# Linear attention and squared-ReLU FFN on one core: softmax sums of four head pairs in one PSUM pair, their inverses spread by DMA from single rows

## The chip, the cores and the metric

The kernel runs on one core of a Trainium2 chip. The metric is the device time of one execution in microseconds. Before the change it is 482.66 us, the median of three runs (481.07 to 483.11).

## The reference

Attention with keys and values projected along the sequence from 1024 to 64 rows, and then a feed-forward layer with a squared ReLU. There are 8 batches of 8 heads, 1024 tokens of 64 elements; 8192 tokens of 512 enter the second part.

```python
k_proj = np.einsum('ks,bhsd->bhkd', E, k)              # 64 rows instead of 1024
v_proj = np.einsum('ks,bhsd->bhkd', F, v)
scores = (1 / np.sqrt(64)) * np.matmul(q, k_proj.transpose(0, 1, 3, 2))
attn = np.exp(scores - scores.max(-1));  attn = attn / (attn.sum(-1) + 1e-9)
x = np.matmul(attn, v_proj)                            # to (8192, 512)
h = np.maximum(x @ w_in, 0.0)                          # 512 -> 2048
out = (h * h) @ w_out                                  # 2048 -> 512
```

## The kernel before

A batch is split into two chunks of 512 tokens. The feed-forward part is the bulk of the work. It multiplies 2x2 block matrices in seven products instead of eight, so sums of blocks are made on VectorE beforehand: of x (x_sum, by `sum_x`), of h (`s12`, `s4`, by `sum_h`), and of the weights once. In the steady state two generators run side by side. `firsts` issues, step by step, one of the seven products of a group (four matmuls of 256 columns, line 652), and `seconds` issues one quantum of the second layer of the chunk before (four matmuls of 256 columns, line 572). A batch has 56 such steps, 28 a chunk. TensorE's order is written by hand; the order of the other engines follows from a list scheduler that works with the buffers' release.

The attention of the next batch is put between these steps by a plan: `on(step, b, name)` puts a method of batch b's `Attention` at that step. Per batch it consists of

- `load_kv`, `load_q`: loads on GpSimd's queue, into one buffer each for K, V and Q
- `project` (line 254): 16 matmuls give k and v projections in one PSUM bank; two kp copies of 64 rows for each half and one half of vp go through VectorE, the other half of vp through ScalarE
- `transpose_k_dma`, `transpose_q_dma`: DMA transposes on SP's queue
- `scores` for each of four head pairs: four matmuls into a pair of PSUM banks, and one Exp on ScalarE gives e, 128x1024 bf16
- `sums_spread(pr)` (line 376), once for two head pairs: see below
- `values(pr)` (line 396): four matmuls into the PSUM pair, and two multiplications by rs on VectorE give xT.

In the steady state all of these share a single pair of PSUM banks (`turn["pairs"] = 1`), so each block must wait until the one before has been read. In `sums_spread` eight matmuls with a 64x32 block of ones sum e over the keys, for two head pairs; each sum comes out on 32 equal rows. Ln and then Exp(-x) on ScalarE give `inv`, 128x1024 f32. Eight DMAs on SP's queue, each of 32 rows of 4 KB, spread these rows to two tiles `rs` of 128x1024, one for a head pair, so that every one of the 64 rows of a head has its inverse. `inv` and `rs` share three buffers.

The same queue of SP carries the stores of the outputs (line 566, 256 KB each, from three buffers o_sb) and the transposes. The buffers u of `part_pool` keep partial products that ScalarE copies out of PSUM (line 544), five of them.

The plan of a batch, with t the step at which batch b's first chunk begins in the first layer's stream: scores 0 to 2 of batch b+2 at t+44, t+47 and t+53, the sums of pairs 0 and 1 at t+50, scores 3 at t+57, the sums of pairs 2 and 3 at t+59, and values at t+63, t+66, t+76 and t+79; `project` of batch b+2 at t+30. The first batches run in a different, plainer order, and batches 2 to 7 go through `sums_spread`.

Of the kernel before, what the change touches and what calls it, by code (L numbers as in the profile page):

```python
# [9 lines left out]
P = 128  # L10
F32 = mybir.dt.float32
BF16 = mybir.dt.bfloat16
# [3 lines left out]
LO, HI = slice(0, 64), slice(64, 128)  # L16
# [3 lines left out]
def kernel(  # L20
# [11 lines left out]
    nc = tc.nc  # L32

    B, H, S, D = q.shape
# [3 lines left out]
    DM = moe_w_out.shape[1]  # L38
# [6 lines left out]
    TCH = S // 2  # L45
# [10 lines left out]
    const_pool = ctx.enter_context(tc.tile_pool(name="const", bufs=1))  # L56
# [4 lines left out]
    soft_pool = ctx.enter_context(tc.tile_pool(name="soft", bufs=3))  # L61
    x_pool = ctx.enter_context(tc.tile_pool(name="x", bufs=2))
    form_pool = ctx.enter_context(tc.tile_pool(name="form", bufs=1))
    part_pool = ctx.enter_context(tc.tile_pool(name="part", bufs=5))
    out_pool = ctx.enter_context(tc.tile_pool(name="outp", bufs=3))
    psum = ctx.enter_context(tc.tile_pool(name="ps", bufs=1, space=bass.MemoryType.PSUM))
    turn = {"att": 0, "bank": 0, "pairs": 2}

# [6 lines left out]
    def att_psum():  # L75
        turn["att"] += 1
        return pair_psum(turn["att"] % turn["pairs"])

    def bank(shape=(P, 512), dtype=F32, n=None):
        if n is None:  # L80
            turn["bank"] += 1
            n = turn["bank"]
        return psum.tile(list(shape), dtype, tag=f"bank{n % 4}", name="ps_bank")
# [34 lines left out]
    nc.vector.memset(zeros[:], 0.0)  # L118
    ones = const_pool.tile([P, D], BF16, name="ones")
    nc.vector.memset(ones[:], 1.0)  # L120


    W_IN_PIECES = ((0, 2), (2, 4), (4, 8), (8, 12), (12, 16))
# [3 lines left out]
    for j, (lo, hi) in enumerate(W_IN_PIECES):  # L127
        t = wpool.tile([P, NCB, (hi - lo) * P], BF16, name=f"w_in_{lo}")
# [6 lines left out]
    for j in range(WP):  # L135
        if j == WP - 1:
            load(Q0[:, :, 4:8, :], tokens(q, 0, i=slice(4, 8)))
        t = wpool.tile([P, fn, DM], BF16, name=f"w_out_{j}")
# [81 lines left out]
    VALUE_QUADS = ((LO, 0, 0, LO), (HI, 0, 1, HI), (HI, 1, 1, LO), (LO, 1, 0, HI))  # L220

    class Attention:
# [31 lines left out]
        def project(self):  # L254
            ps = att_psum()[:, 0]
            for i in range(NI):
                f, l = i == 0, i == NI - 1
                nc.tensor.matmul(ps[LO, :], lhsT=ET[:, i, :], rhs=self.K[:, :, i, :], start=f, stop=l)
                nc.tensor.matmul(ps[HI, :], lhsT=FT[:, i, :], rhs=self.V[:, :, i, :], start=f, stop=l)
            for g in range(2):  # L260
                self.keep_k(ps[LO, g * C // 2:(g + 1) * C // 2], g)
            self.keep_v(ps[HI, :])
# [110 lines left out]
                    nc.vector.tensor_copy(rs[j][lack:lack + 32], rs[j][have:have + 32])  # L373
                self.rs[pr + j] = rs[j]

        def sums_spread(self, pr):

            ps = att_psum()
            for j in range(2):
                for o, par, a, r in VALUE_QUADS:  # L380
                    c = 32 * (2 * a + j)
                    nc.tensor.matmul(
                        ps[c:c + 32, par], lhsT=ones[r, 0:32], rhs=self.e[pr + j][r, par], start=True, stop=True
                    )
            inv = soft_pool.tile([P, 2, TCH], F32, tag="rs", name="inv")
            nc.scalar.activation(inv[:], ps[:], AF.Ln)
            nc.scalar.activation(inv[:], inv[:], AF.Exp, scale=-1.0)
            for j in range(2):
                rs = soft_pool.tile([P, 2, TCH], F32, tag="rs", name="rs")
                for a in range(2):  # L390
                    have = 32 * (2 * a + j)
                    for to in (64 * a, 64 * a + 32):
                        nc.sync.dma_start(rs[to:to + 32], inv[have:have + 32])
                self.rs[pr + j] = rs

        def values(self, pr, spare=False):

# [40 lines left out]
    class Chunk:  # L438
# [100 lines left out]
                        yield  # L539


        def keep(self, ps):
            u = part_pool.tile([P, DM], F32, name="u")
            nc.scalar.copy(u[:], ps)  # L544
            return u

# [31 lines left out]
        def second_spread(self, second_bank):  # L578
# [21 lines left out]
            yield  # L600
            yield from product(7, chain)
            self.put(1, 1, chain, p5)
            yield
            yield from product(3, other)
# [6 lines left out]
        def second_seven(self, first, chain, other, last=False):  # L611
# [16 lines left out]
            yield  # L628
            yield from product(7, chain)
            self.put(1, 1, chain, p5)  # L630
            yield
            yield from product(3, other)
# [10 lines left out]
    class Group:  # L643
# [35 lines left out]
        def p5(self):  # L679
            self.other = bank(n=turn["bank"] + 2)  # L680
            self.product(5, self.other, True)
            self.kept5 = self.chunk.keep(self.other[:])

        def p6(self):
            self.product(6, self.chain)
            self.u2 = self.chunk.keep(self.chain[:])

        def p2(self):
            self.product(2, self.first)
# [18 lines left out]
    with tc.manual_schedule(engines={PE}):  # L708
# [30 lines left out]
        def at(step, fn, *args, **kwargs):  # L739
            plan.setdefault(step, []).append(lambda: fn(*args, **kwargs))  # L740

        def run(steps, start=0):
            for step, _ in enumerate(steps, start + 1):
                for stage in plan.pop(step, []):
                    stage()
            return step

        def run_all(*parts):
            step = 0
            for part in parts:  # L750
                step = run(part, step)
            assert not plan, plan

        atts = {0: att}
        chunk = {(0, c): Chunk(att, c) for c in range(2)}
# [7 lines left out]
        nxt = atts[1]  # L763
# [42 lines left out]
        nxt = atts[2]  # L806
        at(1, nxt.transpose_k)
        at(3, nxt.scores, 0)
        at(5, nxt.scores, 1)
        at(7, nxt.sums_spread, 0)  # L810
        at(9, nxt.scores, 2)
        at(11, nxt.scores, 3)
        turn["pairs"] = 1
        run_all(chunk[1, 0].first_plain())
        lent.close()
        second_pool = ctx.enter_context(tc.tile_pool(name="ps_second", bufs=1, space=bass.MemoryType.PSUM))
# [37 lines left out]
        def both():  # L854
            f, s = firsts(), seconds()
            for _ in f:
                next(s, None)
                yield

        def on(step, b, name, *args):  # L860
            at(step, lambda: getattr(atts[b], name)(*args))

        for b in range(1, B - 1):
            t = 56 * (b - 1)
            if b > 1:
                on(t + 1, b + 1, "scores", 3)
            on(t + 3, b + 1, "sums_spread", 2)
            on(t + 7, b + 1, "values", 0)
            on(t + 10, b + 1, "values", 1)
            on(t + 20, b + 1, "values", 2)  # L870
            on(t + 23, b + 1, "values", 3)
            for c in range(2):
                at(t + 24, lambda b=b, c=c: chunk[b + 1, c].sum_x())
            if b + 2 < B:
                on(t + 2, b + 2, "transpose_q_dma")
                if b + 3 < B:
                    at(t + 2, begin, b + 3)
                    on(t + 3, b + 3, "load_q")
                on(t + 30, b + 2, "project")
                on(t + 32, b + 2, "transpose_k_dma")  # L880
                if b + 3 < B:
                    on(t + 34, b + 3, "load_kv")
                on(t + 44, b + 2, "scores", 0)
                on(t + 47, b + 2, "scores", 1)
                on(t + 50, b + 2, "sums_spread", 0)
                on(t + 53, b + 2, "scores", 2)
        steps = both()
        run(steps)
        assert not plan, plan
# [31 lines left out]
```

## Time and profile before

| | us |
|---|---|
| median of three runs | 482.66 |
| the profiled execution | 482.35 |
| its span | 480.5 |
| matmuls of the first layer's seven products, line 652, x_sum by w_in_sum (x624) | 93.9 |
| values, matmuls line 405 (x112) | 11.5 |
| scores, matmuls line 329 (x112) | 11.3 |
| copies of the projection on VectorE, lines 246 and 247 (x14 each) | 5.8 and 5.7 |
| copy of half of vp on VectorE, line 252 (x7) | 4.9 |
| multiplications into xT, line 409 (x56) | 36.0, 684 ns each |
| x_sum, four additions, line 150 | 417 and 418 ns each |

"Busy" is the time in which an engine has work; several matmuls can be under way together, so their sum says little, and the starts of neighbouring matmuls tell more. How much of the DMA engines' time the queues take:

```profile
q0 software_dynamic: 30640, 29.23, 39.4%
q1 hardware_dynamic: 49216, 36.97, 29.2%
```

The columns are packets, megabytes, and the share of 16 engines' span. q0 is GpSimd's loads, q1 all that SP issues.

### The profile page before, as it was taken

The page shows a single profiled execution, that of the slowest core. Times are in us where ns is not written, and L with a number is a line of the kernel's source. Part 1 is how long each engine was busy: PE and PEld are TensorE (multiplying, and loading weights), DVE is VectorE, ACT ScalarE, POOL GpSimd, SP SyncE. Part 2 cuts the span into 40 slices and gives each one's busy share as a digit, 9 for nine tenths or more (in the row PEclk, how much of TensorE's full clock was granted, in tenths as well). Part 3 has the DMA queues.
Part 4 walks back from the last instruction along what each step waited for, and adds up shares of the span by engine and source line. Part 5 has one row for each costly group of instructions (what it writes and reads, how often), then busy time and mean ns, then how long its engine had stood idle before and what let it go on. Part 6 is the DMA issues. An engine that isn't in the chain of part 4 may idle for free.

```text
span 480.5 us, 10027 instructions
## 1 busy us (share of the span) xinstructions
PE 470.4 (98%) x4106; PEld 351.5 (73%) x4106; DVE 350.7 (73%) x613; ACT 287.2 (60%) x466; POOL 32.4 (7%) x45
## 2 busy tenths in 40 slices
PE   8999999999999999999999999999999999999996
PEld 3444445537878788787878778887887778888885
DVE  2456897956996679767897579966797678967671
ACT  2464467397547774678546785477745775565641
POOL 7310010200010000100010000100000000000000
PEclk9999999999999999999999999999999999999999
DMA  9999998999949496767939499495811054101012
GB/s 184 204 205 206 221 164 150 168 230 189 197 86 168 122 201 163 119 134 186 196 103 182 93 220 175 96 160 139 203 56 55 23 132 111 67 23 67 24 65 89
DMA packets 80046, 66.98 MB, mean 139 GB/s; under 512 B 30720, under 2 KB 76032, under 8 KB 80000
## 3 DMA queue, kind: packets, MB, share of 16 engines
q0 software_dynamic: 30640, 29.23, 39.4%
q1 hardware_dynamic: 49216, 36.97, 29.2%
q8 instruction: 32, 0.52, 0.4%
q10 hardware_dynamic: 144, 0.13, 0.1%
q14 instruction: 14, 0.11, 0.1%
HBM read 59.24 MB, written 16.78 MB: 158 GB/s over the span
## 4 chain that ended last, share of the span: by engine, by line
PE 71%; DVE 22%; ACT 3%; issue 2%; DMA 1%; DVEq 0%; ACTq 0%
PE ps_bank L652 28%; PE ps_second L572 27%; PE ps_bank L489 6%; DVE h L150 3%; DVE x_sum L150 3%; DVE h L666 3%; DVE s L150 2%; PE ps_att L329 2%; DVE xT L409 2%; PE ps_second L549 2%; PE ps_att L405 2%; DVE kp L246 1%; DVE rs L373 1%; DVE kp L247 1%; DVE w_in_sum L150 1%
## 5 line engine op out<-in xcount | busy, mean ns | idle before, releaser
L150 DVE TENSOR_TENSOR h<-h 128x1024 bf16<-128x1024 bf16 (+1 forms) x182 | 108.0, 616 | 39.1 <-ACT h L662 25.4
L652 PE MATMUL ps_bank<-x_sum,w_in_sum 128*128 128x256 bf16 x624 | 93.9, 273 | 0.0
L652 PEld LDWEIGHTS <-w_in_sum 128*128 128x128 bf16 x832 | 78.7, 98 | 16.2 <-issue 7.5
L572 PEld LDWEIGHTS <-h 128*128 128x128 bf16 x832 | 80.8, 98 | 10.6 <-DVE h L150 0.2
L662 ACT ACTIVATE h<-ps_bank 128x512 bf16<-128x512 f32 x104 | 62.9, 605 | 28.5 <-PE ps_bank L652 28.3
L544 ACT COPY u<-ps_bank 128x512 f32<-128x512 f32 x107 | 63.2, 591 | 26.6 <-PE ps_bank L652 23.6
L666 DVE CUSTOM_DVE_ANT_0 h<-ps_bank,u 128x512 bf16<-128x512 f32 x104 | 68.9, 685 | 13.0 <-PE ps_bank L652 12.5
L652 PEld LDWEIGHTS <-w_in 128*128 128x128 bf16 x624 | 58.8, 98 | 16.2 <-issue 9.5
L677 ACT COPY ps_bank<-ps_bank 128x512 f32<-128x512 f32 x52 | 29.7, 570 | 66.1 <-PE ps_bank L652 66.1
L572 PEld LDWEIGHTS <-s 128*128 128x128 bf16 x624 | 61.0, 98 | 7.1
L652 PE MATMUL ps_bank<-xT,w_in 128*128 128x256 bf16 x416 | 62.5, 273 | 0.0
L572 PE MATMUL ps_second<-w_out_sum,s 128*128 128x256 bf16 x416 | 62.4, 273 | 0.0
L572 PE MATMUL ps_second<-w_out_sum,h 128*128 128x256 bf16 x416 | 62.2, 273 | 0.0
L572 PE MATMUL ps_second<-w_out,h 128*128 128x256 bf16 x416 | 60.3, 273 | 0.0
L409 DVE TENSOR_TENSOR xT<-ps_att,rs 128x512 bf16<-128x512 f32 x56 | 36.0, 684 | 15.9 <-PE ps_att L405 15.9
L489 PE MATMUL ps_bank<-xT,w_in 128*128 128x512 bf16 x192 | 45.3, 379 | 1.8 <-DVE xT L434 1.0
L485 ACT ACTIVATE h<-ps_bank 128x512 bf16<-128x512 f32 x48 | 28.1, 606 | 16.1 <-PE ps_bank L489 15.9
L150 DVE TENSOR_TENSOR o_sb<-ps_second,u 128x512 f32<-128x512 f32 x27 | 18.5, 684 | 25.9 <-PE ps_second L572 20.7
L489 PEld LDWEIGHTS <-w_in 128*128 128x128 bf16 x192 | 17.7, 98 | 24.6 <-issue 6.2
L343 ACT ACTIVATE expT<-ps_att 128x1024 bf16<-128x1024 f32 x32 | 32.9, 1036 | 2.9 <-PE ps_att L329 2.5
L652 PE MATMUL ps_bank<-x_sum,w_in 128*128 128x256 bf16 x208 | 31.4, 273 | 1.4 <-DVE h L666 1.4
L652 PE MATMUL ps_bank<-xT,w_in_sum 128*128 128x256 bf16 x208 | 31.3, 273 | 0.0
(104 smaller groups left out, 477.2 us busy)
## 6 DMA issues: line engine op xcount, KB each, us to landing
out_dram<-o_sb SPq DMA_DIRECT2D x63, 256.0 KB, 2.4
rs<-inv SPq DMA_DIRECT2D x96, 128.0 KB, 2.8
K_sb<-in_k_dram POOLq DMA_DIRECT2D x7, 1024.0 KB, 9.5
V_sb<-in_v_dram POOLq DMA_DIRECT2D x7, 1024.0 KB, 15.8
Q_sb<-in_q_dram POOLq DMA_DIRECT2D x7, 1024.0 KB, 12.6
w_out<-in_moe_w_out_dram POOLq DMA_DIRECT2D x4, 512.0 KB, 17.9
w_in<-in_moe_w_in_dram POOLq DMA_DIRECT2D x3, 512.0 KB, 15.0
k_f<-in_k_dram SPq DMA_DIRECT2D x1, 512.0 KB, 4.9
```

What stands on the lines that cost most here:

```text
L150: return nc.vector.tensor_tensor(out=o, in0=x, in1=y, op=op)
L329: nc.tensor.matmul(ps[o, par], lhsT=self.kT[r, h % 4, h // 4, :], rhs=self.qT[r, h, n, :], start=True, stop=True)
L343: nc.scalar.activation(e[:], ps[:], AF.Exp, scale=SCALE)
L409: nc.vector.tensor_tensor(out=self.xT[:, pr, :, par], in0=ps_x[par].rearrange("p (c t) -> p c t", c=2), in1=rs[:, par].rearrange("p (c t) ...
L485: nc.scalar.activation(h, ps.rearrange("p (a t) -> p a t", a=2), AF.Relu)
L489: nc.tensor.matmul(ps[:], lhsT=w_in_blk(cb, fb), rhs=self.xT[:, cb, self.c].rearrange("p a t -> p (a t)"), start=(cb == 0), stop=(cb == NC ...
L544: nc.scalar.copy(u[:], ps)
L572: nc.tensor.matmul(ps[:, i * HM:(i + 1) * HM], lhsT=self.h_form(n, fb)[:, i * P:(i + 1) * P], rhs=w_out_form(n, fb), start=fresh and i == ...
L652: nc.tensor.matmul(ps[:, j * HC:(j + 1) * HC], lhsT=w_in_form(n, cb, 2 * self.g + j), rhs=self.chunk.x_form(n, cb), start=fresh and j == 0 ...
L662: nc.scalar.activation(self.out(kh, a), ps[:], AF.Relu)
L666: nc.vector._custom_dve(TENSOR_ADD_SAT, out=self.out(kh, a), in0=ps[:], in1=more[:], s0=3.0e38, s1=0.0)
L677: nc.scalar.copy(self.chain[:], self.first[:])
```

## The change

Three things are changed together.

1. `sums_spread` becomes `sums_all`, once a batch, for all four head pairs. The sums of a head pair now come out on 16 rows each: a matrix `pick` has ones in the columns 0 to 15 for the first two pairs and in 16 to 31 for the others, and the matmuls of the others accumulate onto the first. Ln and Exp run once for a batch. `inv` gets a buffer of its own.
2. `spread(pr)` issues four DMAs for a head pair. Each takes one row of one bank of `inv` (512 f32, 2 KB) and writes it to 64 partitions of `rs`.
3. The plan: `project` and the k transpose of batch b+3 at t+49 and t+50 instead of t+86 and t+88, with the loads behind them; `transpose_q_dma` at t+12 instead of t+2, `load_q` at t+26 instead of t+3; scores at t+37, 40, 43, 46; the sums and all four spreads at t+53; values at t+62, 65, 75, 78; the two `sum_x` ten steps apart instead of together. For batch 2 the sums and spreads stand at step 13 of the plain chunk before.

The u buffers become two for those of p5 and p6 in the first layer and two for the second layer's, and o_sb has two buffers instead of three.

```diff
-    part_pool = ctx.enter_context(tc.tile_pool(name="part", bufs=5))
-    out_pool = ctx.enter_context(tc.tile_pool(name="outp", bufs=3))
+    part_pool = ctx.enter_context(tc.tile_pool(name="part", bufs=2))
+    out_pool = ctx.enter_context(tc.tile_pool(name="outp", bufs=2))
...
+    pick = const_pool.tile([P, 2, 32], BF16, name="pick")
+    nc.vector.memset(pick[:], 0.0)
+    for m in range(2):
+        nc.vector.memset(pick[:, m, 16 * m:16 * m + 16], 1.0)
...
-        def sums_spread(self, pr):
+        def sums_all(self):
             ps = att_psum()
-            for j in range(2):
-                for o, par, a, r in VALUE_QUADS:
-                    c = 32 * (2 * a + j)
-                    nc.tensor.matmul(
-                        ps[c:c + 32, par], lhsT=ones[r, 0:32], rhs=self.e[pr + j][r, par], start=True, stop=True
-                    )
-            inv = soft_pool.tile([P, 2, TCH], F32, tag="rs", name="inv")
+            for m in range(2):
+                for j in range(2):
+                    for o, par, a, r in VALUE_QUADS:
+                        c = 32 * (2 * j + par)
+                        nc.tensor.matmul(
+                            ps[c:c + 32, 0 if r == LO else 1], lhsT=pick[r, m], rhs=self.e[2 * m + j][r, par],
+                            start=m == 0, stop=m == 1, skip_group_check=True,
+                        )
+            inv = soft_pool.tile([P, 2, TCH], F32, tag="inv", name="inv", bufs=1)
             nc.scalar.activation(inv[:], ps[:], AF.Ln)
             nc.scalar.activation(inv[:], inv[:], AF.Exp, scale=-1.0)
-            for j in range(2):
-                rs = soft_pool.tile([P, 2, TCH], F32, tag="rs", name="rs")
-                for a in range(2):
-                    have = 32 * (2 * a + j)
-                    for to in (64 * a, 64 * a + 32):
-                        nc.sync.dma_start(rs[to:to + 32], inv[have:have + 32])
-                self.rs[pr + j] = rs
+            self.inv = inv
+
+        def spread(self, pr):
+            rs = soft_pool.tile([P, 2, TCH], F32, tag="rs", name="rs")
+            m, j = divmod(pr, 2)
+            for o, par, a, r in VALUE_QUADS:
+                row = 32 * (2 * j + par) + 16 * m
+                nc.sync.dma_start(
+                    rs[o, par], self.inv[row:row + 1, 0 if r == LO else 1].unsqueeze(1).broadcast_to((1, 64, TCH))
+                )
+            self.rs[pr] = rs
...
-        def keep(self, ps):
-            u = part_pool.tile([P, DM], F32, name="u")
+        def keep(self, ps, tag="second"):
+            u = part_pool.tile([P, DM], F32, name="u", tag=tag)
...
+        def project(step, b):
+            on(step, b, "project")
+            on(step + 1, b, "transpose_k_dma")
+            if b + 1 < B:
+                at(step + 1, begin, b + 1)
+                on(step + 1, b + 1, "load_kv")
+
+        project(24, 3)
         for b in range(1, B - 1):
             t = 56 * (b - 1)
-            if b > 1:
-                on(t + 1, b + 1, "scores", 3)
-            on(t + 3, b + 1, "sums_spread", 2)
-            on(t + 7, b + 1, "values", 0)
-            on(t + 10, b + 1, "values", 1)
-            on(t + 20, b + 1, "values", 2)
-            on(t + 23, b + 1, "values", 3)
+            for pr, step in enumerate((6, 9, 19, 22)):
+                on(t + step, b + 1, "values", pr)
             for c in range(2):
-                at(t + 24, lambda b=b, c=c: chunk[b + 1, c].sum_x())
+                at(t + 23 + 10 * c, lambda b=b, c=c: chunk[b + 1, c].sum_x())
             if b + 2 < B:
-                on(t + 2, b + 2, "transpose_q_dma")
+                on(t + 12, b + 2, "transpose_q_dma")
                 if b + 3 < B:
-                    at(t + 2, begin, b + 3)
-                    on(t + 3, b + 3, "load_q")
-                on(t + 30, b + 2, "project")
-                on(t + 32, b + 2, "transpose_k_dma")
-                if b + 3 < B:
-                    on(t + 34, b + 3, "load_kv")
-                on(t + 44, b + 2, "scores", 0)
-                on(t + 47, b + 2, "scores", 1)
-                on(t + 50, b + 2, "sums_spread", 0)
-                on(t + 53, b + 2, "scores", 2)
+                    on(t + 26, b + 3, "load_q")
+                    project(t + 49, b + 3)
+                for pr in range(4):
+                    on(t + 37 + 3 * pr, b + 2, "scores", pr)
+                on(t + 53, b + 2, "sums_all")
+                for pr in range(4):
+                    on(t + 53, b + 2, "spread", pr)
```

More of the change, by code (lines that the diff above doesn't have):

```diff
@@ L681, in p5 @@
             self.product(5, self.other, True)
-            self.kept5 = self.chunk.keep(self.other[:])
+            self.kept5 = self.chunk.keep(self.other[:], "first")
         def p6(self):
             self.product(6, self.chain)
-            self.u2 = self.chunk.keep(self.chain[:])
+            self.u2 = self.chunk.keep(self.chain[:], "first")
         def p2(self):
@@ L809 @@
         at(5, nxt.scores, 1)
-        at(7, nxt.sums_spread, 0)
         at(9, nxt.scores, 2)
@@ L813, with on @@
         turn["pairs"] = 1
+        def on(step, b, name, *args):
+            at(step, lambda: getattr(atts[b], name)(*args))
+        on(13, 2, "sums_all")
+        for pr in range(4):
+            on(13, 2, "spread", pr)
         run_all(chunk[1, 0].first_plain())
@@ L858, in both @@
                 yield
-        def on(step, b, name, *args):
-            at(step, lambda: getattr(atts[b], name)(*args))
+        def project(step, b):
[5 more added lines that the diff above has]
+        project(24, 3)
         for b in range(1, B - 1):
             t = 56 * (b - 1)
-            if b > 1:
-                on(t + 1, b + 1, "scores", 3)
-            on(t + 3, b + 1, "sums_spread", 2)
-            on(t + 7, b + 1, "values", 0)
-            on(t + 10, b + 1, "values", 1)
-            on(t + 20, b + 1, "values", 2)
-            on(t + 23, b + 1, "values", 3)
+            for pr, step in enumerate((6, 9, 19, 22)):
+                on(t + step, b + 1, "values", pr)
             for c in range(2):
-                at(t + 24, lambda b=b, c=c: chunk[b + 1, c].sum_x())
+                at(t + 23 + 10 * c, lambda b=b, c=c: chunk[b + 1, c].sum_x())
             if b + 2 < B:
-                on(t + 2, b + 2, "transpose_q_dma")
+                on(t + 12, b + 2, "transpose_q_dma")
                 if b + 3 < B:
-                    at(t + 2, begin, b + 3)
-                    on(t + 3, b + 3, "load_q")
-                on(t + 30, b + 2, "project")
-                on(t + 32, b + 2, "transpose_k_dma")
-                if b + 3 < B:
-                    on(t + 34, b + 3, "load_kv")
-                on(t + 44, b + 2, "scores", 0)
-                on(t + 47, b + 2, "scores", 1)
-                on(t + 50, b + 2, "sums_spread", 0)
-                on(t + 53, b + 2, "scores", 2)
+                    on(t + 26, b + 3, "load_q")
[3 more added lines that the diff above has]
+                on(t + 53, b + 2, "sums_all")
+                for pr in range(4):
+                    on(t + 53, b + 2, "spread", pr)
         steps = both()
```

## The prediction

> **What bounds the kernel now.** I read the busy table, then the waits of TensorE, then the timeline around one attention block, and last the DMA views, because the change puts new work there.
>
> ```profile
> PE 470.4 (98%) x4106; PEld 351.5 (73%) x4106; DVE 350.7 (73%) x613; ACT 287.2 (60%) x466; POOL 32.4 (7%) x45
> ...
> L382 PE MATMUL ps_att<-expT,ones 64*32 64x512 bf16 x96 | 4.9, 387 | 0.0
> ...
> L386 ACT ACTIVATE inv<-ps_att 128x1024 f32<-128x1024 f32 x12 | 12.3, 1022 | 0.9 <-PE ps_att L382 0.9
> L387 ACT ACTIVATE inv<-inv 128x1024 f32<-128x1024 f32 x12 | 12.8, 1063 | 0.2
> ```
>
> TensorE is the bound. From 105 to 460 us its waits list one entry:
>
> ```profile
> PE ps_bank L652 <- DVE h L666: 1.4, 5, 0.3
> ```
>
> Five waits, one a batch. The timeline shows their true size: starts of neighbouring quanta are 0.44 us apart, here 0.89, so 0.45 is lost each time, 2.2 us in all. The chain of waits runs through VectorE there, from xT at 186.6 us over x_sum, kp and vp to h.
>
> ```profile
> 200.33 0.60 PE L572 MATMUL ps_second<-w_out,h 128*128 128x256 bf16 x4
> 201.22 0.60 PE L652 MATMUL ps_bank<-x_sum,w_in 128*128 128x256 bf16 x4 [0.29 <-DVE h L666]
> ...
> 157.18 0.60 PE L572 MATMUL ps_second<-w_out,s 128*128 128x256 bf16 x4
> 157.71 0.41 PE L382 MATMUL ps_att<-expT,ones 64*32 64x512 bf16 x8
> 158.05 0.61 PE L652 MATMUL ps_bank<-x_sum,w_in_sum 128*128 128x256 bf16 x4
> ```
>
> The last three lines price a sums block: eight matmuls of 512 columns together delay the next quantum by 0.43 to 0.45 us (158.05 less 157.18, less the quantum's own 0.44).
>
> Now the transfers that turn inverse rows into rs, and what the DMA engines did from 213 to 236 us, in forty slices of 0.575 us:
>
> ```profile
> rs<-inv SPq DMA_DIRECT2D x96, 128.0 KB, 2.8
> ...
> L393 SPq DMA_DIRECT2D rs<-inv x96: 507/588/1776, 103.1 to 401.5; - x96
> ...
> 216.52 6.12 SPq L393 DMA_DIRECT2D rs<-inv  x8
> ...
> DMA  0029000099984059988989999999989994797999
> GB/s 0 0 84 367 5 0 0 0 207 207 214 200 93 7 135 207 207 200 183 326 278 257 209 223 290 291 289 290 267 131 228 242 221 100 66 43 84 196 235 187
> ...
> 217.70:219.00 1.30, 1.30 (x14) 1.17 (x13) 0.41 (x1) 1.17 (x2) 0.00 (x0) 1.00 0.90 205
> ```
>
> The store of 213.67 us, from 128 partitions, reaches 367 GB/s in its slice. The rs copies, from 32 partitions to 32, keep the engines as busy (0.90) and move only about 207. That contrast decides this case.
>
> [...]
>
> **The change part by part.** Work is against the profiled execution's 482.35 us (span 480.5); the three runs' median is 482.66, so an answer in its terms is 0.3 higher, which I neglect.
>
> *Sums.* Before, each batch has two blocks of eight matmuls (12 blocks over batches 2 to 7, 0.45 each). After, one block of sixteen: eight independent tiles and then eight that accumulate into the same tiles. One round of 512 columns costs about 0.21 (four 256-column matmuls take 0.44, so 0.22 for 512 columns). So 0.45 + 0.21 = 0.66 against 0.90, six times: 1.4 us less on TensorE. ScalarE loses six Ln and six Exp, 6 x 2.08 = 12.5 us; it is 60% busy and not on the path, so nothing. The memsets of pick run at the start beside loads: nothing.
>
> *k and v a batch ahead, x_sum split.* The four kp copies and vp (4 x 0.41 + 0.69 = 2.3 us of VectorE) leave the crowded stretch after step t+23, and the second x_sum (4 x 0.42 = 1.7) moves ten steps later. At most 2.2 us come back. The projection's 16 matmuls and its k transpose DMA only move; q's transpose moves to t+12 and still has 25 steps before the scores (landing took 6.5 us). The new wait is sums_all for the copies out of the one PSUM pair, four steps after project; 2.3 us of copies fit in, within 0 to 0.4 us a batch. I count 0.
>
> *Fewer buffers.* Two o_sb instead of three and two plus two u instead of five: nothing while stores land in 2.4 us; no longer so if SP or its rings are held up.
>
> *The spread.* The same number of DMAs, 16 a batch, of the same 128 KB, [...]. But a source is one row, read 64 times: [...] A batch now takes 55.85 us (the stretch that begins with xT at 130.80, 186.64, 242.50). [...] so I take no overlap. The price from both sides: 0.6 us a copy if reading does not bind, 4.82 if it does as stated.
>
> Where it ends: in the trace of before, step t+53 starts at 216.6 us. sums_all starts there; in before inv is complete 2.9 us after the sums start, so with 0.2 for the longer block the first copy issues at 219.8. Its first bytes and its receipt cost some 1.9 (a copy lands in 2.5 in this window, 0.6 of it transfer). The last copy of pair 3 lands 1.9 + 77.1 = 79.0 later, at 298.8, and its two multiplies (2 x 0.68) end at 300.2. On the old pace the multiplies at t+22 would end at 242.8 (before: t+23, 243.8). VectorE works in order: the multiply that waits for rs holds all behind it, relu sums and squares included, and TensorE, which needs those and the single PSUM pair, stops within a few steps. So each batch is 57.4 us later, less 0 to 3 us that TensorE can run ahead, plus about 2 for the three or so stores that share the rings (0.7 each at 367 GB/s): 57. Pair 3's rs needs pair 0's multiplies (three rs buffers), at about 242, long before the rings reach it. Six batches: 342 us.
>
> Sum: 482.35 - 1.4 - 2.2 + 342 = 821 us.
>
> **Rivals.** (a) The row is read fast enough: writing binds, 0.6 us a copy. Then pair 0's rs lands at 219.8 + 4 x 0.6 + 2.5 = 224.7, before its multiplies at about 226, and pairs 1 and 2 are 2 us early as well. The 16 issues hold SP for 16 x 0.59 = 9.4 us; with two o_sb this could cost up to 1 us a batch. Result 482.35 - 3.6 = 479, up to 485. This is the one that isn't slower; it decides from a copy of about 1 us (pair 0's margin of 1.3 us over four copies) downwards. [...] Against it: it needs 218 GB/s out of one partition, [...]. (b) [...] 38.5 us a batch, lateness 1.9 + 38.5 + 1.3 - 23.0 = 19, less 2: 17 x 6 = 103, so 582 us. (c) [...] stores behind the copies in SP's queue hold the two o_sb, which stops puts, and so pair 0's multiplies, before rs does, and the rings run dry before pair 3. Some 15 us more a batch: 910.
>
> **How the numbers follow.** The forecast 0.70 (own range 760 to 880: 47 to 67 us a batch), (a) 0.13, (b) 0.12, (c) 0.05. To hold 8 in 10 the range reaches from 560 to 890, over (b) and the near part of (c). About 0.5% (2.4 us) is what a measurement of this kernel tells from no change. Of (a), 0.08 is faster by more, 0.03 within it, 0.02 slower: faster 0.08, same 0.03, slower 0.89.
>
> **What would show it.** Right: rs<-inv lands in 20 us or more at the median, DMA busy near full with GB/s near 27 in the spread, VectorE's multiply into xT waiting for the DMA of rs some 13 to 17 us four times a batch, TensorE's busy share near 60%. The sums block at about 0.66, and the 0.45 us wait gone, show the small terms. Wrong: copies that land in 3 us, or GB/s of 200 during them; then (a) stands and the whole 342 falls.

## The result, and the profile after

The kernel after the change takes 792.25 us (median of four runs, 789.32 to 797.17) against 482.65 us (four runs, 481.07 to 483.11): a ratio of 1.643, 95% interval 1.634 to 1.653. The profiled execution took 789.32 us, its span is 787.5, so the span grew by 307.0.

The page of the kernel after, in the same order as the one before: busy table, the clock granted to TensorE in forty slices, the queue of SP, the chain that ended last by engine, the group of the multiplications into xT, and the stores and copies from issue to landing.

```profile
PE 520.6 (66%) x4096; PEld 376.3 (48%) x4106; DVE 352.3 (45%) x616; ACT 278.0 (35%) x454; POOL 32.8 (4%) x45
...
PEclk9999995677996668966779867599666796676999
...
q1 hardware_dynamic: 52288, 36.97, 53.3%
...
PE 33%; DMA 28%; SPq 28%; DVE 7%; ACT 2%; issue 1%; POOL 1%; DVEq 0%; POOLq 0%
...
L420 DVE TENSOR_TENSOR xT<-ps_att,rs 128x512 bf16<-128x512 f32 x56 | 37.8, 688 | 245.2 <-DMA rs<-inv 240.4
...
out_dram<-o_sb SPq DMA_DIRECT2D x63, 256.0 KB, 3.0
rs<-inv SPq DMA_DIRECT2D x96, 128.0 KB, 16.2
```

TensorE no longer bounds the kernel: DMA and SP's queue hold 56% of the chain. SP moves the same 36.97 MB as before and now takes 53.3% of the engines' time for it, not 29.2%. VectorE's work is the same (352.3 against 350.7), but it stands idle for 240.4 us ahead of the multiplications, waiting for rs.

The DMA view from 519 to 600 us, slices of 2.025 us, shows a spread beginning at 541.65 us (twelfth slice):

```profile
DMA  0310008993339889889969889889689899797898
GB/s 4 104 33 0 0 0 162 218 266 66 132 19 29 26 24 31 25 25 31 27 27 52 26 25 37 26 26 32 33 70 29 25 27 30 23 27 59 39 29 24
```

The sixteen engines are busy for most of each slice (0.6 to 0.9) and move 23 to 39 GB/s. Three slices lie above that, with 52, 70 and 59. They hold no store, since SP issues none between 541.65 and 600.94 us; they lie where the copies of one head pair give way to those of the next, and *e5* below comes back to them. Before, the same bytes moved at about 207. The timelines of SP and of VectorE in that stretch (a transfer "lands" when the trace shows it complete):

```profile
541.65 59.18 SPq L402 DMA_DIRECT2D rs<-inv  x16
600.94 41.83 SPq L577 DMA_DIRECT2D out_dram<-o_sb  x8
```

```profile
562.49 0.69 DVE L420 TENSOR_TENSOR xT<-ps_att,rs 128x512 bf16<-128x512 f32 x1 [8.28 <-DMA rs<-inv]
563.10 0.68 DVE L677 CUSTOM_DVE_ANT_0 h<-ps_bank,u 128x512 bf16<-128x512 f32 x1
572.20 0.69 DVE L420 TENSOR_TENSOR xT<-ps_att,rs 128x512 bf16<-128x512 f32 x1 [8.42 <-DMA rs<-inv]
```

The sixteen copies occupy SP for 59 us, since an issue that took 0.59 us before now lasts up to 11.9, and the next stores come after them. Each multiplication needs two copies, and two multiplications start 9.7 us apart: 4.85 us a copy. TensorE's three largest waits with one of VectorE's, and what TensorE does after a wait:

```profile
PE ps_att L416 <- DVE xT L420: 121.1, 12, 18.2
PE ps_bank L663 <- DVE h L677: 67.9, 7, 12.0
PE ps_second L583 <- DVE o_sb L154: 53.6, 5, 11.3
...
DVE o_sb L154 <- DMA out_dram<-o_sb: 75.0, 6, 15.5
```

```profile
666.33 0.64 PE L416 MATMUL ps_att<-expT,vp 64*64 64x512 bf16 x4 [13.11 <-DVE xT L420]
666.93 1.01 PE L663 MATMUL ps_bank<-x_sum,w_in 128*128 128x256 bf16 x4
667.74 1.06 PE L583 MATMUL ps_second<-w_out_sum,s 128*128 128x256 bf16 x4
668.59 1.06 PE L663 MATMUL ps_bank<-x_sum,w_in_sum 128*128 128x256 bf16 x4
669.44 0.68 PE L583 MATMUL ps_second<-w_out_sum,s 128*128 128x256 bf16 x4
669.96 0.60 PE L663 MATMUL ps_bank<-xT,w_in 128*128 128x256 bf16 x4
670.40 0.60 PE L583 MATMUL ps_second<-w_out_sum,s 128*128 128x256 bf16 x4
```

The columns of the first fence are total, number and longest. The first two waits are one: on VectorE the sums for h come behind the multiplication that waited 8.28 us for rs (563.10 after 562.49). The third is another. Once in each of batches 3 to 7, VectorE stands idle for 14 to 15.5 us until one of the two o_sb is free, because the store that frees it stands behind the sixteen copies in SP's queue. In the batch shown that store lands at 612.21 us, 0.8 us after the last copy, and the multiplications of pair 3 follow at 612.91. The second fence shows a smaller cost: after 13.11 us of rest the quanta start 0.81 to 0.85 us apart, and 0.44 apart again from 669.96 us on. So TensorE runs at about half its pace for 3.6 us: the clock granted to it is 0.54 from 666.3 to 669.9 us and 1.00 from 670 to 672.

**Where the 307 us lie.** From the landing times in the trace, the first copy of a batch is issued 106.5 us after that of the batch before (mean of five, at 112.45, 220.48, 329.06, 435.56, 541.65 and 644.74 us); it was 55.85. Five times 50.65 is 253. Batch 2's copies start 4.4 us later than the old pace gives (the prediction's 219.8 less twice 55.85); 3.4 of it is a query transpose that held SP from 104.14 to 112.36 us, while the inverse was ready at 109.03. The last spread and what comes after it take 142.8 us, 49.6 more than the old pace leaves for them. From a batch's first issue to its last landing 71.1 us pass (69.8 to 73.2), and from there to the next first issue 35.1.

### The profile page after: what moved, and what is told of

It reads as the page before. It is cut to its first block, busy times and chain, and to the rows that moved or that the text cites. A ratio compares the mean times of both kernels' runs of the same rounds, so it can differ in the third digit from the quotient of the medians.

```text
span 787.5 us, 10054 instructions
## 1 busy us (share of the span) xinstructions
PE 520.6 (66%) x4096; PEld 376.3 (48%) x4106; DVE 352.3 (45%) x616; ACT 278.0 (35%) x454; POOL 32.8 (4%) x45
## 3 DMA queue, kind: packets, MB, share of 16 engines
q1 hardware_dynamic: 52288, 36.97, 53.3%
## 4 chain that ended last, share of the span: by engine, by line
PE 33%; DMA 28%; SPq 28%; DVE 7%; ACT 2%; issue 1%; POOL 1%; DVEq 0%; POOLq 0%
SPq L402 28%; DMA rs<-inv 13%; PE ps_bank L663 13%; PE ps_second L583 13%; DMA out_dram<-o_sb 9%; PE ps_bank L500 2%; DMA Q_sb<-in_q_dram 2%; DMA w_in<-in_moe_w_in_dram 2%; PE ps_att L262 1%; DMA kT<-kp 1%; PE ps_att L333 1%; DVE h L154 1%; DVE xT L420 1%; PE ps_second L560 1%; DVE s L154 1%
## 5 line engine op out<-in xcount | busy, mean ns | idle before, releaser
L663 PE MATMUL ps_bank<-x_sum,w_in_sum 128*128 128x256 bf16 x624 | 108.0, 302 | 67.9 <-DVE h L677 67.9
L420 DVE TENSOR_TENSOR xT<-ps_att,rs 128x512 bf16<-128x512 f32 x56 | 37.8, 688 | 245.2 <-DMA rs<-inv 240.4
L663 PEld LDWEIGHTS <-w_in_sum 128*128 128x128 bf16 x832 | 85.9, 106 | 92.9 <-issue 77.5
L154 DVE TENSOR_TENSOR h<-h 128x1024 bf16<-128x1024 bf16 (+1 forms) x182 | 108.0, 616 | 43.6 <-ACT h L673 29.2
L673 ACT ACTIVATE h<-ps_bank 128x512 bf16<-128x512 f32 x104 | 62.2, 598 | 128.8 <-PE ps_bank L663 127.8
L583 PE MATMUL ps_second<-w_out_sum,h 128*128 128x256 bf16 x416 | 70.3, 298 | 53.6 <-DVE o_sb L154 53.6
L416 PE MATMUL ps_att<-expT,vp 64*64 64x512 bf16 x112 | 14.3, 499 | 121.1 <-DVE xT L420 121.1
L583 PEld LDWEIGHTS <-s 128*128 128x128 bf16 x624 | 69.3, 111 | 15.3
L663 PEld LDWEIGHTS <-w_in 128*128 128x128 bf16 x624 | 64.2, 106 | 20.9 <-issue 8.8
L583 PE MATMUL ps_second<-w_out_sum,s 128*128 128x256 bf16 x416 | 72.8, 304 | 0.0
L154 DVE TENSOR_TENSOR o_sb<-ps_second,u 128x512 f32<-128x512 f32 x27 | 18.5, 686 | 88.6 <-DMA out_dram<-o_sb 74.4
L663 PE MATMUL ps_bank<-x_sum,w_in 128*128 128x256 bf16 x208 | 39.3, 322 | 0.0
L583 PE MATMUL ps_second<-w_out,s 128*128 128x256 bf16 x208 | 37.9, 314 | 0.0
## 6 DMA issues: line engine op xcount, KB each, us to landing
rs<-inv SPq DMA_DIRECT2D x96, 128.0 KB, 16.2
```

What stands on the lines that cost most here:

```text
L154: return nc.vector.tensor_tensor(out=o, in0=x, in1=y, op=op)
L416: nc.tensor.matmul(ps_x[par][o], lhsT=self.vp[r, 2 * pr + a, :], rhs=e[r, par], start=True, stop=True)
L420: nc.vector.tensor_tensor(out=self.xT[:, pr, :, par], in0=ps_x[par].rearrange("p (c t) -> p c t", c=2), in1=rs[:, par].rearrange("p (c t) ...
L583: nc.tensor.matmul(ps[:, i * HM:(i + 1) * HM], lhsT=self.h_form(n, fb)[:, i * P:(i + 1) * P], rhs=w_out_form(n, fb), start=fresh and i == ...
L663: nc.tensor.matmul(ps[:, j * HC:(j + 1) * HC], lhsT=w_in_form(n, cb, 2 * self.g + j), rhs=self.chunk.x_form(n, cb), start=fresh and j == 0 ...
L673: nc.scalar.activation(self.out(kh, a), ps[:], AF.Relu)
```

## The experiments

Each edit is against the kernel after unless another is named. The time of the kernel before on the same chip is 481.8 to 482.8 us in all of them. Where no interval is given, the time is that of one execution.

### Is it the source row? One row, sixteen rows, four rows side by side or four apart

Each sum stands on 16 equal rows, so a copy can read several of them. *e1*: sixteen rows, four times each.

```diff
-  rs[o, par], self.inv[row:row + 1, ...].unsqueeze(1).broadcast_to((1, 64, TCH))
+  rs[o, par], self.inv[row:row + 16, ...].unsqueeze(1).broadcast_to((16, 4, TCH))
```

> The changed kernel, but each of the 16 copies a batch reads the 16 equal rows of its sum, each four times, in place of one row 64 times; destination, bytes, count and order stay. [...] so a copy takes 1.2 us in place of 4.8 and a batch's copies 19 in place of 70; they then end about when the multiplies want them, a delay of 0 to 3 us a batch remains, 480 to 500 us in all. Rival, that a source with a repeat, or 64 pieces of 2 KB where before had 32 of 4 KB, is slow by itself: still about 790. Rival, that the fewer o_sb and u buffers or the moved projection cost the time: still about 790.

*e2*: four neighbouring rows, sixteen times each. *e3*: four rows that lie four apart.

```diff
+  e2: self.inv[row:row + 4, ...].unsqueeze(1).broadcast_to((4, 16, TCH))
+  e3: self.inv[row:row + 16:4, ...].unsqueeze(1).broadcast_to((4, 16, TCH))
```

> The changed kernel, but each copy reads 4 neighbouring equal rows 16 times each, so only 4 DMA engines take part [...] 4.8 us a copy, 750 to 830 us. Rival, that it is the single row (the one partition) that can't be read faster: four rows give four times as much, 1.2 to 1.4 us a copy, and 480 to 510 us. Rival, that sixteen engines quarrel over one row: with four engines much faster as well.

> As e2, but the 4 rows are 4 partitions apart, [...] 1.2 to 1.4 us a copy, 480 to 510 us. Rival, that the count of engines or of rows decides: the same time as e2, whatever that is.

The DMA view of one spread of e2 (slices of 2.025 us), then of e3 (0.6 us), then of e1 (0.6 us). The slices of 86 to 115 in e2, and those above 150 at the end of e3 and e1, hold stores; e1's slices of 184, 229 and 164 lie at borders between pairs:

```profile
DMA  0222222222222222222222222222233522222111
GB/s 10 25 25 25 25 26 25 25 25 26 31 26 33 24 24 25 24 26 25 24 33 31 25 26 25 25 26 25 25 86 93 115 26 24 25 24 39 28 36 28
```

```profile
DMA  0012222222222222322222222222222226759521
GB/s 0 0 61 99 102 99 106 99 99 106 92 92 99 99 102 102 130 99 106 99 106 99 102 99 106 99 102 102 96 109 96 109 96 253 227 167 297 188 96 56
```

```profile
GB/s 3 0 92 89 102 99 102 99 106 96 126 184 109 106 99 92 89 109 229 150 116 109 89 102 96 164 160 99 96 106 102 92 120 273 350 224 21 0 14 270
```

| | rows read | engines' busy share | sixteen copies | a copy, mean | time |
|---|---|---|---|---|---|
| after | 1 | 0.86 | 68.4 | 4.27 | 792.25 |
| e2 | 4, side by side | 0.24 | 79.1 and 79.7 | 4.94 and 4.98 | 852.1 |
| e3 | 4, four apart | 0.2 to 0.3 | 21.1 and 21.3 | 1.32 and 1.33 | 552.22 |
| e1 | 16, side by side | 0.85 | 18.8 and 19.1 | 1.17 and 1.20 | 504.71, ratio 1.048 (1.045 to 1.051) |

The busy share is the mean of sixteen engines over one spread, for e3 in its slices. Sixteen copies are counted from the first packet to the last, in the two last batches, which have no loads beside them. In the kernel after, the mean hides two things: inside a pair the landings are 4.8 us apart, and at the borders between pairs copies overlap (see *e5*).

e2 and e3 differ in nothing but which rows are read: the number of rows and bytes is the same, and so is the busy share, about that of four engines out of sixteen. Rows that lie four apart are read 3.7 times as fast as neighbours. So the time of a copy depends on which rows it reads: some 25 to 27 GB/s from one row or from four neighbours, some 100 from four rows that lie four apart or from sixteen neighbours. Neither the number of rows nor the engines' busy share sets it. e1, which changes only the rows that are read, takes 287.5 us less than the kernel after.

All three times lie above what was expected (480 to 500, 750 to 830 and 480 to 510 us). e3 misses by most: its copies take 29 to 33 us, not 21, in the batches that have loads beside them. What e1 still lacks is taken up below.

### Do copies of two head pairs overlap?

*e5* issues the four copies of pair 0, from rows 0 and 32, and the four of pair 1, from rows 64 and 96, alternately.

```diff
-  for o, par, a, r in VALUE_QUADS:          # spread(pr), one pair
-      nc.sync.dma_start(rs[o, par], ...)
+  for o, par, a, r in VALUE_QUADS:          # spread(0) does pairs 0 and 1
+      for n in (0, 1):
+          nc.sync.dma_start(rs[n][o, par], ...)
```

> The changed kernel with the copies of pairs 0 and 1 issued alternately, [...]; pairs 2 and 3 as they were. The prediction had 'no overlap': all 16 copies end 77 us after they begin, whatever their order, and pair 0 is ready later (after 35 us and not 19), so 800 us or more. Rival, [...] the eight alternating copies take 20 to 30 us in place of the 34 to 38 that two pairs took, and the total falls by 5 to 12 us a batch, to 720 to 765 us.

711.01 us, below the rival's range. The DMA view of one spread, slices of 1.5 us:

```profile
GB/s 9 33 27 51 55 57 57 48 49 66 49 51 59 55 48 53 31 25 37 26 31 26 26 26 30 49 63 34 25 26 27 31 25 26 25 31 116 205 56 161
```

While the two pairs alternate, the rate is 48 to 66 GB/s, about twice that of one row. It falls to 25 to 37 for pairs 2 and 3, which were left one after the other, but for two slices at the border between them (49 and 63). The eight alternating copies have landed 23.9 us after the first issue, where two pairs took 38.3. Pair 0 is ready after 20.9 us, no later than in the kernel after (20.7): the copies between its own cost it nothing. From first issue to last landing this spread takes 56.7 us, not 69.8, and the next one begins 13.6 us earlier.

So copies of the two pairs on one queue do run side by side; whether one engine overlaps two copies, or some engines are a copy ahead of others, these runs don't separate.

The kernel after gets a little of it at each border between pairs. Its slices of 52, 70, 59 and 39 GB/s hold some 227 KB more than 27 GB/s (a copy of 128 KB in 4.8 us) would have moved, and at that rate these would have taken 8.4 us (an estimate from the slices), which is about what its spread is shorter than sixteen copies one after the other. Inside a pair, where the source passes from one row to the row 32 partitions on, no slice rises, and the landings stay 4.8 us apart. Which rows overlap was not shown beyond those that are read here.

### The plan alone

*e4* keeps the plan of the change, with the sums, copies and buffers of the kernel before (blocks of sums at t+53 and t+59).

```diff
-  on(t + 53, b + 2, "sums_all")
-  for pr in range(4):
-      on(t + 53, b + 2, "spread", pr)
+  on(t + 53, b + 2, "sums_spread", 0)
...
+  on(t + 3, b + 1, "sums_spread", 2)
```

> The changed kernel's plan (k and v a batch ahead, x_sum split, scores at t+37 to t+46, values at t+62 to t+78) with the sums, the 32-row copies and the buffers of the kernel before; the two sums blocks stand at t+53 and t+59. What I counted for the plan: 2.2 us less, since the 0.45 us wait a batch goes, so a ratio of 0.995 to the kernel before and 480.3 us. Rival: the wait only moves to another product, or the later q transpose and the projection before the sums bring new ones: 482 to 486.

Far off: 538.99 us, ratio 1.118 (1.116 to 1.120). Its waits, and then GpSimd's and SP's timelines around one batch:

```profile
PE ps_att L409 <- ACT inv L390: 48.3, 6, 13.1
...
ACT inv L390 <- DMA rs<-inv: 40.3, 6, 11.7
```

```profile
243.49 0.88 POOL L89 DMA_DIRECT2D K_sb<-in_k_dram  x1 [65.82 <-PE ps_bank L656]
244.36 0.88 POOL L89 DMA_DIRECT2D V_sb<-in_v_dram  x1
245.62 0.88 POOL L89 DMA_DIRECT2D Q_sb<-in_q_dram  x1 [0.38 <-issue]
```

```profile
249.40 7.67 SPq L397 DMA_DIRECT2D rs<-inv  x8
257.39 0.39 SPq L570 DMA_DIRECT2D out_dram<-o_sb  x1
265.97 8.00 SPq L397 DMA_DIRECT2D rs<-inv  x8
```

In the new plan the projection frees K and V four steps ahead of the sums, so their 2 MB of loads, with Q's 1 MB behind them in GpSimd's queue, set off 4 to 6 us before the copies. The second block's inverse takes the buffer that the first eight copies still read, and TensorE waits for it: 13.1, 10.7, 9.1 and 10.1 us in the four batches that have loads, 2.7 and 2.6 in the two last ones that have none.

Two attempts to move the loads by the plan failed. *e6* is e4, *w1* is e1, with `load_kv` 25 steps later:

```diff
-  on(step + 1, b + 1, "load_kv")
+  on(step + (1 if b == 3 else 26), b + 1, "load_kv")
```

> e4 (the plan with the sums and copies of before) with the loads of k and v 25 steps later, away from the copies of rs. Theory: in e4 the 2 MB of k and v, issued right after the projection at t+49, [...] delay them by 6 to 8 us; this cost four or five batches 7 to 10 us each, and 2.8 us a batch stay (the second inv waits for a buffer, since the two sums stand six steps apart): 539 falls to 495 to 510. Rival, that the loads are harmless and the closer sums alone cost it: 530 to 540.

> e1 [...] with the loads of k and v 25 steps later. Theory: the stalls of 3 to 5 us in the batches with loads go, the one in batch 2, whose copies SP issues late behind a q transpose, stays: 486 to 491 us. Rival, [...] 500 or more.

538.70 us (ratio 1.118, 1.115 to 1.121) and 505.81 us (1.048, 1.046 to 1.050): no change. The order of GpSimd's queue isn't that of the plan; in w1 the loads still came 6 us ahead of the copies of 237.08 us:

```profile
230.96 0.88 POOL L89 DMA_DIRECT2D K_sb<-in_k_dram  x1 [59.12 <-PE ps_bank L663]
231.82 0.88 POOL L89 DMA_DIRECT2D V_sb<-in_v_dram  x1
233.08 0.88 POOL L89 DMA_DIRECT2D Q_sb<-in_q_dram  x1 [0.37 <-issue]
```

So neither of the two runs says anything on the loads. *w2* turns the order round in w1: sums and spreads at t+49, projection at t+53.

> w1 with the sums and copies at t+49 and the projection at t+53, so that rs has four steps more. If a small lateness of rs is left in w1, this takes it away: 1 to 3 us less than w1. If nothing is late in w1, the same as w1 within 0.5%.

517.64 us, ratio 1.073 (1.069 to 1.077): worse than w1, where 1 to 3 us less or the same was expected. TensorE now waits 18.5 us for ScalarE's copies into u, and ScalarE 31.3 for o_sb to be stored. Which step of the move does that, I didn't take apart.

*e8* is e6 with a real hold: K's and V's loads wait for the second multiplication of values(1), and the query transpose is issued behind the copies.

```diff
-  dma = load(t[:], tokens(src, b))
+  dma = load(t[:], tokens(src, b))          # K, V: after the multiply of values(1)
+  tc.add_manual_dep(dma.ins, held.ins.name, ...)
...
+  order.enter_context(tc.issue_after(atts[self.b - 1].copied.ins))
   nc.sync.dma_start_transpose(...)          # q
```

> e6 with two orders made binding: the loads of k and v wait for a multiply at t+65, and the q transposes stand behind the rs copies of the batch before in SP's queue, so that q's load follows too. In e6 the later step in the plan had not moved the loads, since GpSimd's order is the scheduler's: its queue shows K, V and Q issued together a few us ahead of the copies. Theory: 3 MB of loads under the copies cost e4 and e6 some 8 us in each of four batches; 538.7 falls to 490 to 508, with the stalls of 2.8 us from the closer sums left. Rival, that loads don't matter: 530 to 540.

500.88 us, ratio 1.039 (1.034 to 1.044): 38 of e4's 57 us are gone. The copies from issue to landing, first in e4 (243 to 270 us, the first twelve of a batch), then here (220 to 247 us, all sixteen):

```profile
rs<-inv SPq DMA_DIRECT2D x12, 128.0 KB, 7.4
```

```profile
rs<-inv SPq DMA_DIRECT2D x16, 128.0 KB, 2.4
```

All sixteen of e4's batch have a median of 5.7 us. TensorE's waits for the second inverse are now 2.5 to 3.7 us in every batch, much as they were in e4's batches without loads. *w5* is e8 with the blocks of sums nine steps apart again, as in the kernel before, and with the projection four steps later.

```diff
-  on(t + 53, b + 2, "sums_spread", 0)
+  on(t + 50, b + 2, "sums_spread", 0)
...
-  project(t + 49, b + 3)
+  project(t + 53, b + 3)
```

> The plan of the change with the loads held took 500.88 us, with a stall of about 2.8 us per batch left, where the second inverse waits for the first's spread buffer because the two blocks of sums stand six steps apart. Here they stand nine apart, as before the change. If that wait and its slower clock afterwards are what is left, the stalls go and the time is 478 to 484 us, the lower end if the plan saves the 2 us that I forecast for it. If the plan itself costs time (k and v ahead, project in other places), it stays at 495 to 500 us.

491.56 us, ratio 1.019 (1.017 to 1.020), between the two answers: 9.3 us less than e8, and 9 above the kernel before. TensorE's waits in the steady state:

```profile
PE ps_att L417 <- ACT inv L398: 8.1, 6, 1.8
PE ps_bank L664 <- DVE h L678: 2.3, 5, 0.5
```

The wait ahead of values(0) has halved (1.3 us in most batches, not 2.6), and the wait for h, the one that the change was to remove, is back: from start to start, as the prediction measured it, 0.40 to 0.69 us a batch where it was 0.45. The wait behind the first of these is for the Ln that reads the single PSUM pair, with values(0) one step nearer to the sums than in the kernel before (t+62 after t+59, not t+63); that this step is the rest is argued, not tried.

### What e1 still lacks

*w3* puts e8's two holds into w1: sixteen source rows, and no loads under the copies.

> w1 with the same two binding orders. Theory: the first copy of a batch lands 3.3 us after its issue in every batch and not 8 to 9 us in three of them, the stalls of 3 to 6 us at the first multiply go, in batch 2 as well since no q transpose stands ahead of its copies; what is left are the small gains of the plan and of the common sums: 478 to 484. Rival, that loads don't matter: 503 to 507.

517.23 us, ratio 1.073 (1.071 to 1.075): worse. TensorE's wait for the multiplications into xT is all but gone (16.8 us in w1, at most 0.5 at a time here), but the query transpose now runs beside the loads of K and V, which set off at 248.10 us:

```profile
253.51 16.65 SPq L333 DMA_TRANSPOSE qT<-Q_sb  x1
270.25 10.14 SPq L585 DMA_DIRECT2D out_dram<-o_sb  x4
```

```profile
ACT o_sb L581 <- DMA out_dram<-o_sb: 27.0, 5, 8.4
```

It holds SP for 16.65 us where it took 4.61 before; the stores stand behind it, and with two o_sb ScalarE and then TensorE wait for them. In e8 the transposes hold SP as long (16.15 to 17.44 us in the three batches with loads), but e8 has the three o_sb and five u of the kernel before, and no engine waits for a store there. That points to the buffers; it isn't a clean test, since e8 has the sums and copies of before as well. *w4* holds the two loads some 25 us longer, until the multiplication of values(3).

> The held version with sixteen source rows took 517.23 us; here its K and V loads wait for the multiply of values(3) instead of values(1), some 25 us later in the batch, past the query transposes and the stores. If what was left over 482 us is K and V loads landing under a query transpose and under stores, which then hold SP and the two o_sb buffers, the stall at o_sb goes and the time is 479 to 486 us. If those stalls have another cause, or the loads are now late for the projections of the next batch, it stays at 500 to 520 us.

506.11 us, ratio 1.048 (1.044 to 1.051). The transpose at 249.81 us takes 6.12 us and ScalarE's wait for o_sb falls from 27.0 to 4.2, as expected. The time does not follow: V now comes too late for the projection, and TensorE's wait for it is 12.5 of the 23 us that are missing.

```profile
PE ps_att L268 <- DMA V_sb<-in_v_dram: 12.5, 4, 5.0
```

Of the places tried for these 2 MB none is free: ahead of the copies they delay the first landing (8.1 to 9.3 us instead of 3.3 to 3.6 in e1), in the middle they hold the transpose, at the end the projection. No version beat the kernel before.

## Why the prediction was right, and where it was not

**The mechanism.** That the source binds, "one row, read 64 times", is what e1 shows with sixteen rows in its place; that four rows help when they lie four apart, and not as neighbours, is what e3 and e2 show. The size of it, 4.82 us a copy and 77.1 for sixteen, was the author's estimate, which no trace of before showed; it was measured at 4.8 us between landings inside a pair and at 4.94 to 4.98 in e2. Rival (a), that writing binds, needed 0.6 us a copy.

**"I take no overlap" failed.** A batch's copies take 71.1 us from first issue to last landing, not 79.0. e5 shows that copies of two pairs do overlap, and that it is worth 13.1 us when half of them alternate; the plain order gets it at the three borders alone. Rival (b), 38.5 us a batch, stood for a read twice as fast or for copies that overlap, and this is its overlap, in small. It makes the forecast too high by six times 7.9 us, or 47.

**The rest of a batch.** From a spread's last landing to the next first issue the forecast left 57 + 55.85 - 79.0 = 33.85 us, or 33.25 when the 3.6 us of savings are shared over six batches. It took 35.1, which is 11 us more in six batches. Two causes in the trace are of this size, and their shares weren't separated. One is the wait for o_sb: in the batch shown the multiplications of pair 3 end at 614.2 us, where the last copy's landing at 611.4 would have let them end at 612.1. The other is TensorE's clock, 0.90 from 611.43 to 644.74 us, where matmuls fill 31.7 of 33.3 us.

The three differences, 47.4 us less, 11.1 more and the 4.4 of the first transpose, come to 31.9 less than 821; the profiled execution lies 31.7 below. That the forecast came so near is in part luck, since the first two have opposite signs.

**Rival (c) was half right.** It said that stores behind the copies in SP's queue would hold the two o_sb. They do, for 14 to 15.5 us a batch. But this comes after pair 2's multiplications and not ahead of pair 0's, so SP's queue does not run empty, and by the times above a batch loses at most about 2 us to it, not 15. "Fewer buffers: nothing" came with a condition, "no longer so if SP or its rings are held up", and in the kernel after SP is held up.

**The sums** were right: in e1 a block delays the next quantum by 0.65 us (231.94 to 232.59), against 0.66; its sixteen matmuls, of 382 ns at the median, lie within 0.63 us. **"At most 2.2 us come back"** from the plan: nothing came. The wait for h nearly goes in e8 (0.2 us in all), but no run with this plan was faster than before, and in w5, the best of them, it returned.

**"The projection's 16 matmuls and its k transpose DMA only move ... I count 0"** was the worst step, and hidden by the large one. The list of what moves left out the loads of K and V, whose buffers the projection frees, with Q's behind them. Under copies of 0.6 us the plan with these loads costs 57 us (e4), 38 of which go with the hold of the loads and of the transpose (e8). In the kernel after, a spread of the three batches with all 3 MB beside it is only 2 to 3 us longer than one without (71.6 to 73.2, 69.8 for the last two), so slow copies hide what fast ones show. The two runs nearest to rival (a), e1 and e4, took 504.71 and 538.99 us and not its 479 to 485.

**The signs.** The rate, the nearly full engines and TensorE's share (66%, near 60% forecast) came as written. A copy's landing has a median of 16.2 us, not 20, because SP itself is held at the issue (up to 11.9 us). VectorE waits for rs six times a batch for up to 10.7 us, not four times for 13 to 17: each multiplication needs two copies, not a pair's four, and pair 3's wait is hidden behind the one for o_sb.

## What to carry to other kernels

Price a DMA from its reading side as well as from its writing side. Here a copy of one source row to 64 partitions took 4.8 us where 32 rows to 32 had taken 0.6; with the same 64 partitions to write to, sixteen rows as the source took 1.2. If equal rows exist, read several, and measure which: four rows that lie four apart took 1.3 us, four neighbours 4.9. Or alternate copies from rows that were seen to overlap, as those of pairs 0 and 1 did in e5. And when a plan moves a block, follow the buffers it frees: the loads behind them move too, and land on whatever transfer is short and waited for there.

## What was not expected of the hardware

- Copies from rows 0 and 32 and copies from rows 64 and 96, issued in turn on one queue, run side by side: 48 to 66 GB/s against 25 to 37 (e5).
- Inside a pair, copies that keep the engines 0.2 to 0.3 busy are as fast as copies that keep them 0.85 busy, about 100 GB/s (e3 and e1); e1 gains at the borders, where its slices rise above 150.
- A DMA transpose of Q holds its queue for 14.5 to 17.4 us when 2 MB of loads set off 2 to 7 us before it (three batches each of w3, e8 and w5). It held it for 4.61 in the kernel before, and for 6.12 with the loads later (w4).
- Stores behind slow copies on one queue hold back an engine that needs their buffer: VectorE waits 14 to 15.5 us a batch for o_sb in the kernel after.
- Loads on GpSimd's queue hold back the first of SP's copies by some 5 us (8.1 to 9.3 against 3.3 to 3.6 in e1), though they share no queue with it.
